# Scores of a wide attention as eight products in 32x64 tiles instead of four in 32x128 tiles

## The chip, the cores and the metric

The kernel runs on one core of a Trainium2 chip. The metric is the device time of one launch in microseconds (us). The core has five engines with instruction streams of their own: TensorE (PE, matrix products), VectorE (DVE), ScalarE (ACT), GpSimd (POOL) and SyncE (SP, used here to issue transfers). The profile splits TensorE's work into PE, the products, and PEld, the loads of the stationary operand that stand in front of each product.

## The reference

The program computes two attentions over the same 2048 x 576 input and mixes them by a gate. Attention A is recurrent: 64 segments of 32 rows, each with 8 rows of memory ahead of it, and the memory for the next segment is the first 8 rows of this segment's output. Attention B is wide: 32 heads of width 18, all 2048 queries against all 2048 keys.

```python
def _A_ref(x, mem0, Wq, Wk, Wv, Wo, seg_len):
    mem = mem0
    for s in range(n_seg):                       # 64 segments, one after the other
        h = jnp.concatenate([mem, x[:, s * seg_len:(s + 1) * seg_len, :]], axis=1)
        q, k, v = ...                            # 576 -> 32 heads x 128
        p = _softmax(jnp.where(mask, q k^T * scale, -1e9))
        o = (p v) Wo
        mem = o[:, :M, :]                        # M = 8
        outs.append(o[:, M:, :])

def _B_ref(x, wqkv, wo):
    scores = jnp.einsum('bhqd,bhkd->bhqk', q, k) * scale     # 32 heads, width 18
    p = _softmax(scores, axis=-1)
    o = jnp.einsum('bhqk,bhkd->bhqd', p, v)
    return o.transpose(0, 2, 1, 3).reshape(B, S, D) @ wo

g = _sigmoid((x * gate_w).sum(-1, keepdims=True))
return g * a + (1 - g) * b
```

## The kernel before

**The wide attention, B.** Heads go in groups of four (`GB` = 8 groups), each padded from 18 to 32 rows, so that four heads fill 128 partitions. Queries go in chunks of `QC` = 512, keys in blocks of 128. One such pair of a query chunk and a key block, for four heads, is a *visit*; there are 8 x 4 x 16 = 512 of them (loops over `gq` and `kb`, from line 915). A visit has three parts:

- `visit` (lines 926 to 935): four products, one for each head. Head j has its keys in rows 32j to 32j + 31 of `kch` and its queries in the same rows of `qch`. The stationary operand is 32 rows x 128 keys, the moving one 32 rows x 512 queries, and the result 128 keys x 512 queries. The array is used as four row tiles, `tile_position=(32 * j, 0)`, so the four products can be in it together. Heads 0 to 2 go to the three banks of the tile `sb` in PSUM (the accumulator memory), head 3 to a bank of its own, `sp`.
- `expo` and `expo4` (lines 939 to 945): ScalarE takes the exponential of `sb` (128 x 1536) and of `sp` (128 x 512) into `etb`.
- `values` (lines 950 to 960): four products in column tiles of 128 x 32, added up in `ob` over the sixteen key blocks of a query chunk.

There is one `sb` (three banks), one `ob`, and four banks `pb` that everything else shares, `sp` among them.

**The recurrent attention, A.** For each segment (loop from line 1242): projections to queries, keys and values in column tiles (`project`, products at line 1312, written to `pvv`), copies out of PSUM (`tm`), transposes by transfer (`tt`), scores (`psh`, lines 1426 and 1434), exponential, sums (`pss`), reciprocal (`rq`), a broadcast (`prb`), weighted values (`pso`, line 1500, tiles of 64 x 128), output projection (`acc`, line 1194) and the fold back to the next memory (`pw`). The last rows of segments are projected in units of four banks (`last_unit`, lines 1025 and 1029), and dummy products keep the array busy (`warm_col`, line 902).

**What sets the order.** The class `Plan` holds every piece of work with its engines, an assumed duration and a priority, and works out one order for each engine before a program exists. The visits are put in between the steps of the recurrence. The piece named `sb` (line 937) has the assumed duration 0.3, the mode "row", and takes the default of 4 pairs for the planner's count of instructions. The change touches the body of `visit` alone, so the planner sees the same pieces with the same numbers and every engine keeps its order.

Of the kernel before, what the change touches and what calls it, by code (L numbers as in the profile page):

```python
# [110 lines left out]
class Plan:  # L111
# [59 lines left out]
    def add(  # L171
        self, name, engs, dur, fn, deps=(), prio=5.0, mode=None, take=(), give=(), tail=0.0, dmas=0, kb=0.0,
        use=None, pairs=4, alt=None, waits=0.0,
    ):
        op = Op(name, engs, dur, fn, deps, prio, mode, take, give, tail)
        op.dmas, op.kb = dmas, kb
        op.pairs, op.alt, op.form, op.waits = pairs, alt, mode, waits
        op.kind = self.kinds.setdefault(kind_of(name), len(self.kinds))
        op.use = self.ARRAY.get(mode) if use is None else use
        op.seq = len(self.ops)  # L180
        op.slots = {}
        self.ops.append(op)
        return op
# [193 lines left out]
def kernel(  # L377
# [15 lines left out]
    nc = tc.nc  # L393
    P = nc.NUM_PARTITIONS
# [77 lines left out]
    for j in range(4):  # L472
        r = slice(32 * j, 32 * j + 32)
# [52 lines left out]
    def bank(shape, dt, name, k=0):  # L526
        return ps_a.tile(shape, dt, name=name, tag=f"pb{plan.slot('pb', k)}")

    def given(pool, tag, shape, dt):
        k = plan.slot(tag)  # L530
        return pool.tile(shape, dt, name=tag, tag=f"{tag}{k}", bufs=1)
# [332 lines left out]
    def load_k(c):  # L864
        g, kc = divmod(c, NQC)
        use = visits.get(("kuse", c - NKR))


        def fn(e):
            by_head(ktd, g, slice(kc * QC, (kc + 1) * QC), kring[c % NKR], False, queue(e))  # L870

        k_of[c] = add(f"lk{c}", *carrier(4, c >= 4), fn, [use, z_k[c % NKR], *stores_for(1, g, [kc]), weight_loads["wk"][-1] if c >= 4 else None], prio=0.6, dmas=4, kb=90)

    def load_v(c):
        g, kc = divmod(c, NQC)
        use = visits.get(("vuse", c - NVR))
        hf = g // (GB // 2)

        def fn(e):
            queue(e)(  # L880
                out=vring[c % NVR][:, :].rearrange("p (k f) -> p k f", f=P),
                in_=vgd[hf][4 * kc:4 * kc + 4][:, :, g % (GB // 2), :].rearrange("k p f -> p k f"),
            )

        deps = [v_stores[hf * NKB + kb] for kb in range(4 * kc, 4 * kc + 4)]
        v_of[c] = add(f"lv{c}", *(("POOL", 0.77) if c >= 4 else carrier(1, False)), fn, [use, *deps, weight_loads["wk"][-1] if c >= 4 else None], prio=0.65, dmas=1, kb=128)

    def load_q(i):
        g, qc = divmod(i, NQC)
        use = visits.get(("quse", i - NQR))  # L890

        def fn(e):
            by_head(qtd, g, slice(qc * QC, (qc + 1) * QC), qring[i % NQR], False, queue(e))

        q_of[i] = add(f"lq{i}", *carrier(4, i >= 2), fn, [use, z_q[i % NQR], *stores_for(0, g, [qc]), weight_loads["wk"][-1] if i >= 2 else None], prio=0.55, dmas=4, kb=90)
# [19 lines left out]
    for gq in range(GB * NQC):  # L915
        RANK.update(RANKS[gq // 8])
        g, qc = divmod(gq, NQC)
        load_q(gq)
        for kb in range(NKB):
            c = 4 * g + kb // KC  # L920
            o = (kb % KC) * P
            if qc == 0 and kb % KC == 0:
                load_k(c)
                load_v(c)

            def visit(e, c=c, gq=gq, o=o, kb=kb):
                box["sb", gq, kb] = sb = ps_s.tile([P, 3, QC], FP32, name="sb")
                box["sp", gq, kb] = sp = bank([P, QC], FP32, "sp")
                kc, qt_ = kring[c % NKR], qring[gq % NQR]
                for j in range(4):  # L930
                    r = slice(32 * j, 32 * j + 32)
                    nc.tensor.matmul(  # L932
                        sb[:, j, :] if j < 3 else sp[:, :], lhsT=kc[r, o:o + P], rhs=qt_[r, :], start=True, stop=True,
                        tile_position=(32 * j, 0),
                    )

            vi = add(f"sb{gq}.{kb}", "PE", 0.3, visit, [k_of[c], q_of[gq], last_vi], prio=-0.6 if gq < 2 else 0.0, mode="row", take=("sb", "pb"))

            def expo(e, gq=gq, kb=kb):
                box["etb", gq, kb] = etb = given(bint, "etb", [P, 4, QC], BF16)  # L940
                nc.scalar.activation(out=etb[:, 0:3, :], in_=box["sb", gq, kb][:, :, :], func=ACT.Exp, scale=scale_b)  # L941

            def expo4(e, gq=gq, kb=kb):
                etb = box["etb", gq, kb]
                nc.scalar.activation(out=etb[:, 3, :], in_=box["sp", gq, kb][:, :], func=ACT.Exp, scale=scale_b)  # L945

            ex = add(f"ex{gq}.{kb}", "ACT", act_time(1536), expo, [vi], prio=0.0, take=("etb",), give=(("sb", vi, 0),))
            ey = add(f"ey{gq}.{kb}", "ACT", act_time(512), expo4, [ex], prio=0.01, give=(("pb", vi, 0),))

            def values(e, c=c, gq=gq, kb=kb, o=o):  # L950
                if kb == 0:
                    box["ob"] = ps_o.tile([P, QC], FP32, name="ob")
                ob, vc, etb = box["ob"], vring[c % NVR], box["etb", gq, kb]
                for j in range(4):
                    nc.tensor.matmul(  # L955
                        ob[32 * j:32 * j + 32, :], lhsT=vc[:, o + 32 * j:o + 32 * j + 32], rhs=etb[:, j, :],
                        start=(kb == 0), stop=(kb == NKB - 1), tile_position=(0, 32 * j), skip_group_check=True,
                    )
                if kb == NKB - 1:
                    box["ob", gq] = ob  # L960

            va = add(
                f"ob{gq}.{kb}", "PE", 0.216, values, [ex, ey, v_of[c], last_va], prio=-0.5 if gq < 2 else RANK["ob"], mode="col",
                take=("ob",) if kb == 0 else (), give=(("etb", ex, 0),),
            )
            visits[gq, kb] = (vi, ex, va)
            last_vi, last_va = vi, va
            if kb == 0:
                plan.opens.add(va)
            if kb == NKB - 1:  # L970
                plan.closes.add(va)
            if kb == 0:
                first_va = va
            if kb == NKB - 1:
                visits["quse", gq] = vi
            if qc == NQC - 1 and kb % KC == KC - 1:
                visits["kuse", c], visits["vuse", c] = vi, va

        NBK = QC // 32

        def f_turn(e, gq=gq):
            box["tq", gq] = tq = bint.tile([P, NBK, 32], FP32, name="tq")
            nc.vector.transpose(out=tq[:, :, :].rearrange("p b e -> p (b e)"), in_=box["ob", gq][:, :])

        def f_rec(e, gq=gq):
            box["rtb", gq] = rtb = bint.tile([P, NBK, 1], FP32, name="rtb")
            nc.vector.reciprocal(out=rtb[:, :, :], in_=box["tq", gq][:, :, DhB:DhB + 1])

        def f_mul(e, gq=gq):
            box["tn", gq] = tn = bint.tile([P, NBK, 32], BF16, name="tn")  # L990
            nc.vector.tensor_tensor(
                out=tn[:, :, :], in0=box["tq", gq][:, :, :],
                in1=box["rtb", gq][:, :, :].to_broadcast([P, NBK, 32]), op=ALU.mult,
            )

        def f_back(e, gq=gq):
            box["stage", gq] = stage = bint.tile([P, QC], BF16, name="stage", bufs=2)
            nc.vector.transpose(out=stage[:, :], in_=box["tn", gq][:, :, :].rearrange("p b e -> p (b e)"))  # L998

        prev = fin_state.get("back")  # L1000
        f1 = add(f"ft{gq}", "DVE", 0.7, f_turn, [va, prev], prio=0.5, give=(("ob", first_va, 0),))
        f2 = add(f"fr{gq}", "DVE", 0.26, f_rec, [f1], prio=RANK["fin"])
        f3 = add(f"fm{gq}", "DVE", 0.7, f_mul, [f2], prio=RANK["fin"])
        store2 = stages.get(gq - 2)
        f4 = add(f"fb{gq}", "DVE", 0.7, f_back, [f3, store2], prio=RANK["fin"])
        fin_state["back"] = f4
        if gq < GB * NQC - 1:
            def f_store(e, gq=gq, g=g, qc=qc):
                by_head(otd, g, slice(qc * QC, (qc + 1) * QC), box["stage", gq], True, queue(e))

            stages[gq] = add(f"fs{gq}", *carrier(4, True), f_store, [f4], prio=0.9, dmas=4, kb=90)
        else:
            stages[gq] = f4
# [696 lines left out]
    for n in range(NT):  # L1710
        qc, i = divmod(n, 4)
# [84 lines left out]
```

## Time and profile before

| | |
|---|---|
| time, median of 3 runs | 1423.44 us (1421.48 to 1425.37) |
| the profiled execution | 1421.8 us, of which the span on the core is 1420.0 us |
| PE busy | 1345.2 us, 95% of the span |
| ACT busy | 1091.4 us, 77% |
| DVE busy | 848.2 us, 60% |
| POOL busy | 535.4 us, 38% |
| products of `visit` | 2048, 386 ns each in the profile |
| granted TensorE clock, mean | 0.992 |

Busy time of PE is the union of overlapping products, and the end of a product is modelled, so that 386 ns of one product is not what it takes from the array: the distance from one start to the next is. A line of the groups names the line of the kernel, the engine, the operation, output and inputs by their names, the tile of the array (rows*columns), the shape and the count; then busy time, mean duration of one, and what the engine waited for just before. A line of the timeline gives the start, the length and how many instructions were merged.

### The profile page before, as it was taken

Reading aid. Unit: us, or ns where it says so; the run is one execution under the profiler, and the core shown is the slowest. Engines: PE = TensorE matmul, PEld = TensorE weight load, DVE = VectorE, ACT = ScalarE, POOL = GpSimd, SP = SyncE. Lnnn points to the kernel's source line nnn. Section 1 sums busy time; section 2 is a strip of 40 time slices with the busy share of each in tenths; the row PEclk is TensorE's granted clock in tenths of the full one; section 3 lists DMA queues with packets and bytes.
Section 4 is the critical chain, followed back from the end, with each engine's and each line's share of the span. In section 5 each row is a group of like instructions: output and inputs, shape, how many; then the busy total and the mean of one; then the engine's idle time right before and its main releaser. Section 6 shows DMA issues by size and latency. Waiting matters only on the chain. (4 is left out here: it accounts for less than half of the span.)

```text
span 1420.0 us, 74484 instructions
## 1 busy us (share of the span) xinstructions
PE 1345.2 (95%) x33172; PEld 720.4 (51%) x33184; DVE 848.2 (60%) x2019; ACT 1091.4 (77%) x1277; POOL 535.4 (38%) x1162
## 2 busy tenths in 40 slices
PE   7999899999999999999999999999999999999998
PEld 4555344555554545555555544555554545444545
DVE  4443466665565566656666655656656665665566
ACT  3477688888887787887887888787778788887884
POOL 7352154334532346332543425333354324521310
PEclk9999999999999999999999999999999999999999
DMA  8787544333433344333433334333335333333335
GB/s 251 253 314 220 131 87 75 64 68 69 82 62 64 60 79 76 76 61 65 85 67 70 69 66 76 68 62 69 65 80 89 60 54 59 72 56 53 56 81 169
DMA packets 343997, 130.73 MB, mean 92 GB/s; under 512 B 296495, under 2 KB 330023, under 8 KB 343675
## 3 DMA queue, kind: packets, MB, share of 16 engines
q1 hardware_dynamic: 315155, 80.47, 29.2%
q0 software_dynamic: 26368, 43.31, 11.4%
q8 instruction: 259, 4.24, 1.3%
q10 hardware_dynamic: 2152, 2.19, 0.5%
q14 instruction: 63, 0.52, 0.1%
HBM read 52.74 MB, written 31.12 MB: 59 GB/s over the span
## 5 line engine op out<-in xcount | busy, mean ns | idle before, releaser
L941 ACT ACTIVATE etb<-sb 128x1536 bf16<-128x1536 f32 x512 | 743.5, 1452 | 227.5 <-PE sp L932 153.0
L540 DVE CAST tm<-pvv 128x512 bf16<-128x512 f32 x358 | 246.3, 688 | 230.3 <-PE pvv L1312 228.3
L945 ACT ACTIVATE etb<-sp 128x512 bf16<-128x512 f32 x512 | 305.0, 596 | 4.8 <-PE sp L932 4.8
L1312 PEld LDWEIGHTS <-ht 128*32 128x32 bf16 x7680 | 202.8, 96 | 196.2 <-issue 21.6
L932 PE MATMUL sb<-qch,kch 32*128 32x512 bf16 x1536 | 201.8, 386 | 3.2 <-ACT etb L941 1.8
L932 PE MATMUL sp<-qch,kch 32*128 32x512 bf16 x512 | 197.6, 386 | 7.6 <-DVE vl L540 5.8
L955 PE MATMUL ob<-etb,vch 128*32 128x512 bf16 x2048 | 201.9, 387 | 0.3 <-issue 0.3
L1194 PE MATMUL acc<-wo,ot 128*32 128x288 bf16 (+1 forms) x6144 | 165.7, 248 | 7.3 <-issue 3.6
L1312 PE MATMUL pvv<-wq_m,ht 128*32 128x512 bf16 x2048 | 142.1, 380 | 3.9 <-DVE ht L1559 1.5
L1312 PE MATMUL pvv<-wv_m,ht 128*32 128x512 bf16 x2048 | 141.7, 380 | 0.3 <-DVE tm L540 0.2
L1312 PE MATMUL pvv<-wk_m,ht 128*32 128x512 bf16 x2048 | 140.5, 380 | 0.1
L1194 PEld LDWEIGHTS <-ot 128*32 128x32 bf16 x6144 | 112.7, 97 | 47.0 <-DVE ot L540 17.7
L540 DVE CAST ot<-pso 128x320 bf16<-128x320 f32 x200 | 91.6, 484 | 58.3 <-PE pso L1500 57.3
L932 PEld LDWEIGHTS <-kch 32*128 32x128 bf16 x2048 | 54.5, 91 | 137.0 <-issue 121.7
L1411 DVE COPY qk<-tt 128x512 bf16<-128x512 bf16 x256 | 79.9, 314 | 54.5 <-DMA tt<-tm 51.2
L1261 POOL COPY ht<-xg 128x96 bf16<-128x96 bf16 x64 | 17.7, 277 | 236.8 <-PE pvv L1312 230.5
L955 PEld LDWEIGHTS <-vch 128*32 128x32 bf16 x2048 | 53.6, 94 | 73.5 <-issue 62.5
L851 POOL DMA_DIRECT2D qch<-qtd x120 | 61.7, 521 | 68.3 <-PE sp L932 64.6
L851 POOL DMA_DIRECT2D otd<-stage x124 | 62.8, 513 | 65.0 <-DVE stage L998 38.6
L540 DVE CAST vl<-pv 128x512 bf16<-128x512 f32 x84 | 57.2, 685 | 38.8 <-PE pv L1025 21.8
L1489 DVE TENSOR_TENSOR et<-et,prb 128x320 bf16<-128x320 bf16 x128 | 61.6, 484 | 28.0 <-PE prb L1478 23.1
L1444 ACT ACTIVATE et<-psh 128x320 bf16<-128x320 f32 x128 | 56.6, 445 | 27.0 <-PE psh L1434 25.7
(161 smaller groups left out, 1968.1 us busy)
## 6 DMA issues: line engine op xcount, KB each, us to landing
xl<-qkd SPq DMA_DIRECT2D x64, 128.0 KB
v_sb<-tm SPq DMA_DIRECT2D x256, 32.0 KB
qkd<-vl POOLq DMA_DIRECT2D x48, 128.0 KB, 2.5
wo<-in_A_Wo_dram POOLq DMA_DIRECT2D x4, 1152.0 KB, 10.9
vgd<-vt SPq DMA_DIRECT2D x32, 128.0 KB
wv_m<-in_A_Wv_dram POOLq DMA_DIRECT2D x4, 1024.0 KB
wq_m<-in_A_Wq_dram POOLq DMA_DIRECT2D x4, 1024.0 KB, 9.2
wk_m<-in_A_Wk_dram POOLq DMA_DIRECT2D x4, 1024.0 KB
```

The source lines that it names most:

```text
L540: nc.vector.tensor_copy(out=out_of(), in_=in_of())
L851: dma(out=rows_, in_=pads) if out else dma(out=pads, in_=rows_)
L932: nc.tensor.matmul(sb[:, j, :] if j < 3 else sp[:, :], lhsT=kc[r, o:o + P], rhs=qt_[r, :], start=True, stop=True, tile_position=(32 * j, 0),)
L941: nc.scalar.activation(out=etb[:, 0:3, :], in_=box["sb", gq, kb][:, :, :], func=ACT.Exp, scale=scale_b)
L945: nc.scalar.activation(out=etb[:, 3, :], in_=box["sp", gq, kb][:, :], func=ACT.Exp, scale=scale_b)
L955: nc.tensor.matmul(ob[32 * j:32 * j + 32, :], lhsT=vc[:, o + 32 * j:o + 32 * j + 32], rhs=etb[:, j, :], start=(kb == 0), stop=(kb == NKB - ...
L1194: nc.tensor.matmul(acc[32 * q:32 * q + 32, :], lhsT=o[:, slot, t0:t0 + CT], rhs=wo[:, h, d:d + n], start=(first and s_ == (s_ % 2 if wide ...
L1261: nc.gpsimd.tensor_copy(out=ht[:, 0:NF, M:CT], in_=xg[:, 0:NF, t])
L1312: nc.tensor.matmul(pv[32 * j:32 * j + 32, :], lhsT=ht[:, cc, :], rhs=rw, start=(c == 0), stop=(c == NF), tile_position=(0, 32 * j), skip_g ...
L1411: eng.tensor_copy(out=opened["qk"][:, hf, a, 0:16 * L].rearrange("p (j i t) -> p j i t", i=4, t=L)[:, :, :, 0:CT], in_=box["tt", s, a, hf] ...
L1444: nc.scalar.activation(out=opened["et", hf][:, :], in_=box["psh", s, hf][:, :], func=ACT.Exp, scale=scale_a)
L1489: nc.vector.tensor_tensor(out=et[:, :], in0=et[:, :], in1=box["prb", s, hf][:, :], op=ALU.mult)
```

## The change

The four products of a visit become eight. The 128 keys of a block are taken in two halves of 64: the outer loop goes over the halves, the inner one over the four heads. Each product has a stationary operand of 32 rows x 64 keys, the same moving operand of 32 x 512 queries as before, and writes 64 partitions of the bank that its head had before. The array is used as eight tiles of 32 x 64, `tile_position=(32 * j, i)`. What is computed, where it ends up, the tiles in memory and the order of all pieces are the same. `skip_group_check=True` tells the program builder not to compare the two halves' accumulation groups; it is no instruction.

```diff
-                for j in range(4):
-                    r = slice(32 * j, 32 * j + 32)
-                    nc.tensor.matmul(
-                        sb[:, j, :] if j < 3 else sp[:, :], lhsT=kc[r, o:o + P], rhs=qt_[r, :], start=True, stop=True,
-                        tile_position=(32 * j, 0),
-                    )
+                for i in range(0, P, 64):
+                    for j in range(4):
+                        r = slice(32 * j, 32 * j + 32)
+                        nc.tensor.matmul(
+                            sb[i:i + 64, j, :] if j < 3 else sp[i:i + 64, :], lhsT=kc[r, o + i:o + i + 64], rhs=qt_[r, :],
+                            start=True, stop=True, tile_position=(32 * j, i), skip_group_check=True,
+                        )
```

## The prediction

> **What bounds the kernel now.** I read the page's busy shares first, then the costliest groups, then the stages, then who waits for the changed line, and last the timeline of one visit.
>
> ```profile
> PE 1345.2 (95%) x33172; PEld 720.4 (51%) x33184; DVE 848.2 (60%) x2019; ACT 1091.4 (77%) x1277; POOL 535.4 (38%) x1162
> ...
> L932 PE MATMUL sb<-qch,kch 32*128 32x512 bf16 x1536 | 201.8, 386 | 3.2 <-ACT etb L941 1.8
> L932 PE MATMUL sp<-qch,kch 32*128 32x512 bf16 x512 | 197.6, 386 | 7.6 <-DVE vl L540 5.8
> L955 PE MATMUL ob<-etb,vch 128*32 128x512 bf16 x2048 | 201.9, 387 | 0.3 <-issue 0.3
> ```
>
> TensorE is full. The stages say the same: from 150 to 1350 us it is busy 1150.5 of 1200 us, so only 49.5 us are idle in the body. The changed products start almost without a wait (3.2 and 7.6 us in 512 visits), so what they take is taken from the bounding engine. From the list of waits:
>
> ```profile
> PE psh L1434 <- DVE qk L1411: 10.5, 24, 1.0
> PE prb L1478 <- DVE rq L1470: 8.3, 20, 1.0
> ...
> PE sb L932 <- ACT etb L941: 1.8, 8, 0.4
> ```
>
> The columns are total us, times, longest. PE waits for ScalarE's exponentials 8 times in 512 visits; the other way round ScalarE waits 293 times, 153.0 us, for `sp`. ScalarE is no bound. The stretch of one visit in the timeline gives the price that counts, start to start:
>
> ```profile
> 700.90 0.39 PE L1312 MATMUL pvv<-wq_t,ht 128*32 128x512 bf16 x4
> 701.22 0.10 PEld L932 LDWEIGHTS <-kch 32*128 32x128 bf16 x4 [0.42 <-issue]
> 701.22 0.39 PE L932 MATMUL sb<-qch,kch 32*128 32x512 bf16 x3
> 701.23 0.38 PE L932 MATMUL sp<-qch,kch 32*128 32x512 bf16 x1
> ...
> 701.55 1.05 PE L1312 MATMUL pvv<-wk_m,ht 128*32 128x512 bf16 x16
> ...
> 702.42 0.39 PE L1312 MATMUL pvv<-wk_t,ht 128*32 128x512 bf16 x4
> ...
> 702.64 0.39 PE L955 MATMUL ob<-etb,vch 128*32 128x512 bf16 x4
> ```
>
> Four products of 512 columns in four column tiles take 0.22 us when the next round has the same tile form (702.42 to 702.64). Where the form changes they take 0.32 (700.90 to 701.22), and a visit's round 0.33 (701.22 to 701.55). So the four products of a round do run together, and a change of form costs about 0.1 us on either side of a visit. The trace's own starts inside the round are 3.3 ns apart, tile after tile, in row and in column form.
>
> One more resource matters, since the change adds instructions. The view of the transfers has the program's own loading, and the timeline shows one place where it is late:
>
> ```profile
> q8 instruction: 259, 4.24, 1.3%
> ```
>
> ```profile
> 366.77 0.42 PE L1194 MATMUL acc<-wo,ot 128*32 128x288 bf16 x5
> 368.07 0.55 PE L1194 MATMUL acc<-wo,ot 128*32 128x288 bf16 x11 [0.88 <-issue]
> ```
>
> 4.24 MB in 259 transfers is 16.4 KB each; over TensorE's 66,400 records it is 64 bytes for one. So this queue carries TensorE's program, 256 instructions at a time. The bracket is TensorE in the middle of a sum, waiting for nothing but its next instructions. Numbered in order, the starts with such a gap fall on the same place in each 256. Measured from one such place to the next, a block of 256 took 4.64 us in the median, one in four took under 4.02, one in twenty under 3.55, and the shortest 3.07. Starts of these transfers are never under 3.28 us apart, one in ten under 3.62. That is the pace at which blocks arrive, and TensorE already runs near it in places.
>
> **What the Trainium skill says.** "TensorEngine Tiling (Array Packing)", Key Properties: different tiles load and multiply in parallel, and changing the form drains the array. The trace agrees: 0.22 against 0.32 us. "TensorE: Matmul & The Clock Gate", Measured speedup vs the span model: each further tile adds about 4 ns, up to sixteen tiles of 32x32; the trace has 3.3 ns for four, and no 32x64 tile. The same page, Weight-path perf modes: a fast weight load needs a stationary operand of all 128 columns. The trace agrees in form, since before, the 128 columns are read as 4 chunks of 32. "Runtime: NRT & Kernel Launch", Terms: instruction memory is refilled in 16 KiB blocks; the trace has 16.4 KB.
>
> **The change part by part.**
>
> *Arithmetic.* None is removed. Eight tiles of 32x64 fill the same array as four of 32x128, for the same 512 columns: 213 ns at full clock. Cost 0 if all eight stream together.
>
> *Starts.* Four more pairs in a visit, at 3.3 ns: the last starts 13.3 ns later. The whole round ends later by that, and so does what follows.
>
> *Weights.* After a change of form the loads can't run ahead. The view has no 64-column load. Behind a change, a round of 32-column loads delays its first round by 10 ns (226 against 216 ns to the next), and the 128-column loads in four chunks end alike. Sixty-four columns without chunks are twice 32, so an estimate is 10 ns more. Bounds: 0, if the pairs' 13 ns cover it, and 40, if a column took 1/1.2 ns as the skill's clock page has it in LDWEIGHTS (53 ns for 64, less 13 now); the trace's 10 ns for 32 columns speaks against the latter. I take 10.
>
> *Change of form.* Still one ahead of and one behind each visit. From the last start to the next form's first load, less the streaming, the trace has 91 to 95 ns after column tiles, 94 after the full array, 99 after these row tiles (86 in some), 87 after 64x128. Neither fewer columns nor fewer rows shortens it by more than some ns, so I take 0; bounds -27 ns (64 columns fewer to cross at 2.4 a ns) and +10.
>
> *Sum for one visit.* 13.3 + 10 + 0 = 23.3 ns. The stages of the changed line put 156 of its 2056 load records, 39 visits, ahead of 150 us, where transfers have a share of 0.79 and 0.84 and TensorE waits for them; I count nothing there. 473 x 23.3 ns = 11.0 us.
>
> *Program.* 512 visits x 8 records = 4096 instructions, 16 more blocks on 259, at 6% more instructions for each us. I laid 8 more starts into each visit in the trace's own list of starts, moved what follows by 30 ns, and added up by how much blocks of 256 fall short of the refill's pace. At a pace of 3.6 us the list of before is short by 2.8 us and the new one by 11.2, so 8.4 more; at 3.5 us it is 1.5 and 7.4, so 6 more; at 3.8 us 7.9 and 23.2, so 15 more. I take 8. Low end 2: products already queued cover shortfalls under 0.2 us.
>
> *Who waits.* ScalarE's exponential starts some 25 ns later, within its 227.5 us of idle time ahead of line 941. If that cover went, 512 x 25 ns = 12.8 us would lie on ScalarE. Queued behind the visit on TensorE are the recurrence's projections and `ob`; they come late by the same amount. SP's and POOL's orders are untouched. DVE's copies only wait longer for `pvv` (228.3 us already).
>
> *What is absorbed.* Where TensorE then waits for DVE anyway, a longer visit shortens the wait. `psh` waits in 24 of 128 cases, `prb` in 20 of 128, other lines more rarely. I take 12% of 11.0 + 8, so 2.3 us.
>
> Sum: 11.0 + 8 - 2.3 = 16.7 us. The profiled execution is 1421.8 us (span 1420.0 and 1.8 around it) and would be 1438.5. The median of the runs is 1.6 us above that execution: 1423.4 + 16.7 = **1440 us**.
>
> **Rivals.**
>
> *The two halves don't stream together.* Both halves of a head need the same 32 rows. If their products excluded each other, each visit would take a second round: 512 x 0.216 = 110.6 us, so 1534 us. For it: no tile of this form is in the trace. Against it: column tiles share all 128 rows among four products, start 3.3 ns apart and finish a round in 0.216 us; the skill's sixteen tiles split rows and columns at once.
>
> *Nothing that can be measured.* The starts are covered by the change of form, the program's loading keeps up, and the rest goes into TensorE's 49.5 us of idle time: under 4 us, 1424 to 1427. For it: the absolute numbers are small, and blocks take 4.64 us in the median. Against it: those 49.5 us are spread over 1200, while the visits are everywhere.
>
> *Faster.* The drain could be shorter for a tile of 64 columns, on the side behind the visit. At the bound, -27 ns, the visit would gain 3.7 ns (13.3 + 10 - 27), 2 us in all. To win it must be shorter by more than the 23.3 ns and what the program's loading costs, 8 us over 473 visits or 17 ns: from about 40 ns on. At 60 ns less, 20 ns x 473 = 9 us, so 1414 us. Against it: 91 to 99 ns after four different forms.
>
> **How the numbers follow.** A measurement of this kernel tells about 0.3%, 4.3 us, from no change. My forecast, 1428 and up without a second round, has 0.76; two rounds 0.06; no measurable change 0.10; faster 0.08. So slower is 0.82. In the forecast's own case the low ends (13.3 ns a visit and 2 us of loading, less 12%) give 7 us, 1431, and the high ends (13.3 + 40 + 10 ns and 15 us, less 12%) 40 us, 1463; both high at once is unlikely. The range is 1426 to 1458: it leaves out two rounds, faster, part of no change, and a few hundredths above.
>
> **What would show it.** Line 932 should be 4096 products of tile 32*64, with starts about 3.3 ns apart. From a visit's first start to the next form's first start there should be about 0.35 us instead of 0.33; 0.54 would be two rounds, 0.30 a shorter drain. The instruction queue should carry 275 transfers, and "issue" should show more idle time ahead of lines 1194, 1312, 1434 and 1500, on products without a wait of their own. ACT and DVE busy times should stay. I am wrong if the visit's price is unchanged, if the blocks cost nothing, or if the waits for DVE shrink by as much as the visits grow.

## The result, and the profile after

The median went from 1424.4 us (four runs, 1421.48 to 1429.11) to 1443.09 us (four runs, 1440.49 to 1448.58): a ratio of 1.0133, 95% interval 1.0092 to 1.0174, or 18.7 us slower. The profiled execution after took 1448.6 us (span 1446.8), 5.5 us above that median.

The page of the changed kernel: busy shares, the instruction queue, and the groups of the changed line (now 933; everything below the edit stands one line lower).

```profile
PE 1361.7 (94%) x35219; PEld 738.6 (51%) x35232; DVE 846.8 (59%) x2019; ACT 1093.8 (76%) x1277; POOL 535.4 (37%) x1162
...
q8 instruction: 275, 4.51, 1.4%
...
L933 PE MATMUL sb<-qch,kch 32*64 32x512 bf16 x3072 | 224.3, 400 | 7.5 <-DMA kch<-ktd 4.5
L933 PE MATMUL sp<-qch,kch 32*64 32x512 bf16 x1024 | 213.5, 399 | 4.4 <-DVE vl L540 4.2
```

The eight tiles are there (32*64, 3072 + 1024 products), and the program takes 275 blocks. The busy times of DVE, ACT and POOL stay within 3 us. TensorE has 16.5 us more busy time in a span that is 26.8 us longer, so it also stands still longer. This is the timeline of the same visit as before the change, the 250th:

```profile
714.97 0.39 PE L1313 MATMUL pvv<-wq_t,ht 128*32 128x512 bf16 x4
715.29 0.41 PE L933 MATMUL sb<-qch,kch 32*64 32x512 bf16 x3
715.30 0.40 PE L933 MATMUL sp<-qch,kch 32*64 32x512 bf16 x1
715.30 0.41 PE L933 MATMUL sb<-qch,kch 32*64 32x512 bf16 x3
715.32 0.40 PE L933 MATMUL sp<-qch,kch 32*64 32x512 bf16 x1
715.64 1.05 PE L1313 MATMUL pvv<-wk_m,ht 128*32 128x512 bf16 x16
```

Both halves start within 0.03 us and share one round; ahead of the visit the change of form takes the same 0.32 us, behind it the next form starts 0.35 us after the visit's first product in place of 0.33. Over all 512 visits the trace's own starts give, from the first product to the next form's first load, a median of 350 ns in place of 323. Those 27 ns are 13 of later starts (first to last product 23 in place of 10) and 14 from the last start to the next form (327 in place of 313). I call this the visit's price.

The list of TensorE's waits holds the waits for the next instructions, marked "issue". First the largest of them before, then the list after:

```profile
PE acc L1194 <- issue: 3.6, 2, 2.8
```

```profile
PE psh L1435 <- DVE qk L1412: 9.2, 20, 1.2
PE prb L1479 <- DVE rq L1471: 9.1, 18, 1.2
PE acc L1195 <- issue: 6.2, 10, 1.6
...
PE sb L933 <- ACT etb L942: 1.4, 6, 0.3
```

All lines marked "issue" come to 5.1 us before and to 13.4 us after. TensorE waits for ScalarE's exponential (`etb`) only 6 times, so ScalarE is still no bound.

Each weight load outside the visits has its counterpart in the other trace, in the same order (31,136 of them), so I compared the gaps between them. The profiled execution after is 26.5 us longer from the first to the last: 14.9 us in gaps that hold a visit, 11.5 us in the others. Of the latter, those after 150 us come to 12.6 us: +17.2 us in stretches of twelve records, each at a border between two blocks of 256, -5.0 us where a border lay before, and 0.4 us everywhere else. Such a stretch holds 4.7% of the starts. Laying the stretches a little differently moves these sums by about 1 us. So outside the visits the loss lies at the borders. The waits say the same: if weight loads, products and semaphore records are numbered together, all 19 of this trace's "issue" waits after 160 us end at places 192 to 195 of a block of 256. In all twelve traces of this case together it is 168 of 168.

### The profile page after: what moved, and what is told of

It is laid out like the page before. It is cut to its first block, busy times and chain, and to the rows that moved or that the text cites. A ratio compares the mean times of both kernels' runs of the same rounds, so it can differ in the third digit from the quotient of the medians.

```text
span 1446.8 us, 78579 instructions
## 1 busy us (share of the span) xinstructions
PE 1361.7 (94%) x35219; PEld 738.6 (51%) x35232; DVE 846.8 (59%) x2019; ACT 1093.8 (76%) x1277; POOL 535.4 (37%) x1162
## 5 line engine op out<-in xcount | busy, mean ns | idle before, releaser
L942 ACT ACTIVATE etb<-sb 128x1536 bf16<-128x1536 f32 x512 | 743.8, 1453 | 253.3 <-PE sp L933 183.5
L933 PE MATMUL sb<-qch,kch 32*64 32x512 bf16 x3072 | 224.3, 400 | 7.5 <-DMA kch<-ktd 4.5
L933 PE MATMUL sp<-qch,kch 32*64 32x512 bf16 x1024 | 213.5, 399 | 4.4 <-DVE vl L540 4.2
L933 PEld LDWEIGHTS <-kch 32*64 32x64 bf16 x4096 | 70.7, 101 | 148.0 <-issue 130.5
```

The source lines that it names most:

```text
L933: nc.tensor.matmul(sb[i:i + 64, j, :] if j < 3 else sp[i:i + 64, :], lhsT=kc[r, o + i:o + i + 64], rhs=qt_[r, :], start=True, stop=True, t ...
```

## The experiments

Ten runs were made besides the two. A ratio is to the kernel before in the same sitting. The sittings differ by up to 0.8% (the median of the kernel before was 1415.5 to 1427.1 us in the three of them), so sums over whole traces from different sittings are compared with care, and ratios decide. Microseconds given after a ratio are worked out from it; where the two medians differ by another amount, that is given too.

**Instructions without tiles: `halves`.** Eight products again, but in the old form, with each head's queries taken as two halves (against the kernel before).

```diff
-                for j in range(4):
-                    r = slice(32 * j, 32 * j + 32)
+                for h in range(0, QC, 256):
+                    for j in range(4):
+                        r, q = slice(32 * j, 32 * j + 32), slice(h, h + 256)
...
+                            sb[:, j, q] if j < 3 else sp[:, q], lhsT=kc[r, o:o + P], rhs=qt_[r, q],
+                            start=True, stop=True, tile_position=(32 * j, 0), skip_group_check=True,
```

> Eight products in a visit as after the change, but in the old row tiles of 32x128: each head's 512 queries are taken as two halves of 256 columns. The instructions grow by the same 4096, the tiles don't change. Theory (half of the loss is the program's loading, the other half the tiles): a visit's price, start to next form's start, stays within 5 ns of 323, so under 2.5 us; the loading costs 6 to 14 us as in the changed kernel, less a little that waits take up. Expected 8 to 12 us over before, ratio 1.006 to 1.008, with 275 transfers of instructions and issue waits of some 10 us in place of 5. Rival (all of the loss lies in the form of the tiles, 26 us over 512 visits is 52 ns each): no change beyond 2 us, ratio under 1.002.

Measured: 1444.57 us, ratio 1.0134 (1.0111 to 1.0156), 19 us (17.5 by the medians). The visit's price is 325 ns, 2 more than before or 1.0 us in all. This stretch of its timeline shows it from 711.11 to 711.43. The waits for instructions add up to 15.2 us, of which the second view has the largest part:

```profile
710.78 0.39 PE L1313 MATMUL pvv<-wq_t,ht 128*32 128x512 bf16 x4
711.11 0.28 PE L933 MATMUL sb<-qch,kch 32*128 32x256 bf16 x3
711.12 0.28 PE L933 MATMUL sp<-qch,kch 32*128 32x256 bf16 x1
711.23 0.27 PE L933 MATMUL sb<-qch,kch 32*128 32x256 bf16 x3
711.24 0.27 PE L933 MATMUL sp<-qch,kch 32*128 32x256 bf16 x1
711.43 1.05 PE L1313 MATMUL pvv<-wk_m,ht 128*32 128x512 bf16 x16
```

```profile
PE acc L1195 <- issue: 6.5, 12, 1.5
```

So some 17 us come from 4096 more instructions alone, about twice what I had expected of them. Outside the visits its starts are 15.6 us later at borders of blocks. Some 7 us more lie elsewhere outside the visits; the kernel before was also 5.3 us slower in this sitting (1427.1 us) than in the trace that it is compared with (1421.8 us). The rival, that all lies in the tiles, falls.

**Visits' price without instructions: `ninetysix`.** The other way round: four products, with a longer load of the stationary operand.

```diff
+                if "sb" not in box:
+                    box["sb"] = ps_s.tile([P, 3, QC], FP32, name="sb")
+                box["sb", gq, kb] = sb = box["sb"]
...
+                    w = 96 if j < 3 and (gq or kb) else P
-                        sb[:, j, :] if j < 3 else sp[:, :], lhsT=kc[r, o:o + P], rhs=qt_[r, :], start=True, stop=True,
+                        sb[0:w, j, :] if j < 3 else sp[:, :], lhsT=kc[r, o:o + w], rhs=qt_[r, :], start=True, stop=True,
```

> The kernel before with four products in a visit and not one instruction more, but three of the four stationary operands have 96 columns in place of 128 (the last quarter of the keys is left out for three heads, after the first visit; the tile sb is one tile for good, so that these rows hold old scores). 96 columns are no longer read in four chunks. If loading goes column by column at 2.4 a ns, it takes 40 ns in place of 13, so the visit's price is 350 ns as in the changed kernel, without its instructions. Theory (the visit's price costs what it is, less what waits take up): 11 to 14 us over before. Rival (the loading of the program alone makes the loss, a visit's 27 ns go into waits): under 5 us. If the price stays at 323, the chunks aren't what the changed kernel lost.

Measured: ratio 1.0038 (1.0024 to 1.0052), 5.4 us, with 22 runs of it. The price is 347 ns, 24 more than before, and the instruction queue carries 259 transfers as before. The page's groups show the form, and that its products hardly wait:

```profile
L935 PE MATMUL sb<-qch,kch 32*96 32x512 bf16 (+1 forms) x1536 | 215.7, 412 | 3.8 <-ACT etb L944 1.9
```

512 x 24 ns = 12.3 us, of which 5.4 (3.4 to 7.4) arrive at the end. Neither expectation was met: the visits do cost, but some 55% of their price goes, where the prediction took off 12%. Where it goes stays open. TensorE's waits other than for instructions are 45.2 us here and 55.4 in the trace of before, but the two are from different sittings, and this profiled execution (1415.64 us) was itself 5.4 us under the median of its runs.

**Where the borders lie: `shift48` and `shift128`.** The kernel before, with products of one column at the gate that move all later instructions; the second kernel has 128 in place of 48.

```diff
+        for k in range(48):
+            nc.tensor.matmul(pgs[:, 0:1], lhsT=xT[:, 0, 0:P], rhs=gw[:, 0:1], start=True, stop=True)
```

> The kernel before with 48 more products of one column, at the gate (about 50 us after the start), each written over by the gate's own products. They cost 48 x 26 ns = 1.2 us of TensorE where they stand and move every later instruction by 96 places against the blocks of 256 in which the program is loaded. Theory (loading stalls where a block is used up in less than about 3.5 us): replaying the starts of before with boundaries moved by 96 gives 12.1 us of shortfall in place of 1.5 at a pace of 3.5 us, so 10 us more; with the 1.2 us and what waits take up, 7 to 12 us over before, ratio 1.005 to 1.008. Rival (where the blocks' borders lie doesn't matter): at most the 1.2 us, ratio under 1.001.

> The same with 128 more products: 128 x 26 ns = 3.3 us where they stand, and 256 places, so the borders of the blocks fall on the same instructions as before. Theory: no more shortfall than before, so between 0 and 3.5 us over before, and less than the one with 48, though 80 products more are in it. Rival (instructions cost by their number alone): more than the one with 48.

Measured: with 48, ratio 1.0066 (1.0041 to 1.0092), 9.4 us (7.8 by the medians); with 128, ratio 1.0034 (1.0011 to 1.0057), 4.8 us (2.6 by the medians). In the traces, gaps after 150 us grew by 13.8 us with 48 and by 1.4 us with 128, where the rest of the loss lies ahead of 150 us, at the gate itself. So eighty more of these products cost less, as the theory has it: they leave the borders on the same instructions. The intervals of the two ratios overlap; the traces tell them apart. With 48, "issue" waits after 160 us number 14 in place of 4. They still end at places 192 to 195, which now means at other instructions. From the two lists of waits, with 48 first:

```profile
PE psh L1436 <- issue: 2.6, 2, 1.4
PE pv L1031 <- issue: 2.0, 3, 0.9
```

```profile
PE pgs L815 <- issue: 2.5, 1, 2.5
PE pv L1031 <- issue: 0.5, 1, 0.5
```

The 2.5 us in the second are at the gate, where 128 products in a row wait for the next block. I had expected at most 3.5 us of this kernel and had not thought of this wait; whether the limit was passed depends on the measure (4.8 or 2.6 us).

**Which part of the tile costs: `sixteen`.** Sixteen tiles of 32x32 (against the changed kernel).

```diff
-                for i in range(0, P, 64):
+                for i in range(0, P, 32):
-                            sb[i:i + 64, j, :] if j < 3 else sp[i:i + 64, :], lhsT=kc[r, o + i:o + i + 64], rhs=qt_[r, :],
+                            sb[i:i + 32, j, :] if j < 3 else sp[i:i + 32, :], lhsT=kc[r, o + i:o + i + 32], rhs=qt_[r, :],
```

> Sixteen products of 32 rows x 32 keys in a visit. Starts: twelve more than before at 3.3 ns, so the last starts 50 ns after the first in place of 10 (before) and 23 (after the change). Weights: if the 14 ns that the changed kernel has between the last start and the next form's first load, over the old form, come from loading 64 columns one by one, 32 columns give 313 ns again (as before) and the visit's price is 363 ns; if any column tile has them, 327 stays and the price is 377 to 380. On 473 to 512 visits that is 19 to 29 us. Program: 12288 more instructions, 48 more blocks; replaying the starts at a pace of 3.5 to 3.6 us for a block gives 24 to 32 us more. Expected 40 to 60 us over before, 1465 to 1485 us. Rival (the tiles alone): 20 to 29 us, 1445 to 1453.

Measured: 1479.76 us, ratio 1.0392 (1.0363 to 1.0421), 56 us (52.7 by the medians). One visit of its trace, without the products in between:

```profile
728.82 0.39 PE L933 MATMUL sb<-qch,kch 32*32 32x512 bf16 x3
...
728.87 0.38 PE L933 MATMUL sp<-qch,kch 32*32 32x512 bf16 x1
729.18 1.05 PE L1313 MATMUL pvv<-wk_m,ht 128*32 128x512 bf16 x16
```

The price is 363 ns in the median, and from the last start to the next form it takes 313 ns, as with the old tiles. So a tile of fewer columns doesn't cost these 14 ns as such. That they are the changed kernel's 64 columns, loaded one by one, fits this run; loading and draining were not measured apart. The visits' 40 ns come to 20 us at most. So more than half of the 56 us is again the program, as the expectation had it; its 307 blocks have waits for instructions of 22.9 us.

**The order of the tiles: `inner`** (against the changed kernel).

```diff
-                for i in range(0, P, 64):
-                    for j in range(4):
+                for j in range(4):
+                    for i in range(0, P, 64):
```

> The changed kernel with the two loops of a visit exchanged: the two halves of a head stand one after the other, so two tiles on the same 32 rows start back to back. Theory (each further tile 3.3 ns, the columns' loading 14 ns, whatever the order): a visit's price of 350 ns, 1440 to 1446 us, within 4 us of the changed kernel. Rival (tiles on the same rows hold each other up): the price rises by 14 ns and more.

Measured: 1437.77 us, ratio 1.0161 (1.0131 to 1.0191), price 350 ns. In that sitting the kernel before took 1415.5, so this is 22 us more; the interval overlaps that of the changed kernel. The time itself is under the 1440 to 1446 us expected, in a sitting whose kernel before was 9 us faster than in the first. Two tiles on the same 32 rows that start back to back don't hold each other up: the price is the same.

**The changed kernel again: `again`.**

> The changed kernel once more, beside the others: 16 to 21 us over before. Theory: where the shortfall at the blocks' borders lies differs from one execution to the next by some us, since the refills' pace does, while the visits' price of 350 ns doesn't.

Measured: ratio 1.0147 (1.0111 to 1.0183), 21 us (21.9 by the medians), at or just above the upper end of what was expected; price 350 ns. At the borders its gaps are 8.6 us longer than before, where the first profiled execution had 12.5; in `inner` it is 7.6. In these three executions the price is the same and the borders vary.

**Both with a program made shorter: `lean_four`, `lean_eight`, `lean_halves`.** Half of the recurrent scores are left out, which takes away as many instructions as the change adds; the visits are those of before, of the change, and of `halves`.

```diff
-                for r in range(8):
+                for r in range(0, 8, 2):
                     for i in range(4):
                         k, o = (i // 2) * 8 + r, 32 * (i % 2)
```

> The kernel before with every other step of the recurrent scores left out (16 of the 32 score products of each of 128 pieces; those heads keep the mask's values alone, so this part of the result is missing). It has 2048 products and as many weight loads less, 16 blocks of the program less, which is what the change adds. Expected 10 to 25 us under before: at most 2048 x 11 ns of the array, and fewer waits for the program. It is the base for the next run.

> The changed kernel with the same part left out, so its number of instructions is that of the kernel before. Theory (two prices that add: 27 ns for each visit and the loading): the loading is relieved, the visits' price is still there, so 12 to 16 us over lean_four, with a visit's price of 350 against 323 ns. Rival (the loading alone decides, and a longer visit only takes up time that the loading would have taken): under 6 us over lean_four.

> lean_four (half of the recurrent scores left out) with the visits as eight products of 256 columns in row tiles of 32x128, so the instructions of lean_eight at a visit's price of some 326 ns. Theory: with the program's loading relieved the 4096 instructions cost little, 1 to 5 us over lean_four, and the 11.5 us of lean_eight over lean_four are the price of its visits. Rival (what lean_eight lost is still loading): as much as lean_eight, 9 to 14 us over lean_four.

Measured, against the kernel before: `lean_four` 0.9958 (0.9943 to 0.9973), `lean_eight` 1.0034 (1.0017 to 1.005), `lean_halves` 1.0008 (0.9989 to 1.0026). `lean_four` is 5.7 us under before; I had expected 10 to 25, and why it is less stays open. `lean_eight` is 11.5 us over `lean_four` in the same sitting, a little under the 12 to 16 expected. `lean_halves`, from another sitting, is over `lean_four` by 1.0008 / 0.9958 = 1.0050, some 7 us, with an uncertainty of about 3.4 us from the two intervals. That lies between its two expectations. The same 4096 instructions cost less in the shorter program (19 us for `halves` falls to 7). What is left of `lean_eight`'s 11.5 us for the form of its tiles is the ratio of its ratio to that of `lean_halves`, 1.0026 or 3.7 us, with an uncertainty of some 3.5 us; that agrees with the 5.4 us of `ninetysix`. The traces don't show what the 7 us are: at borders the lean kernels' gaps differ by 1 to 2 us only, and the profiled executions of `lean_four` and `lean_halves` by 1.8 us in all.

## Why the prediction was right, and where it was not

The sum was 16.7 us and the result 18.7; 1440 stands against 1443.09, inside 1426 to 1458. The sign and the two causes, a longer visit and more instructions to load, hold. That the sum came within 2 us is luck: what the program costs was put at about half, what is absorbed of the visits' price was put much too low, and the two errors offset each other in part. The two later sets of runs of this form (`again`, `inner`) came to 21 and 23 us.

- **Arithmetic and tiles: right.** Eight tiles stream together; the second round (1534 us) didn't come, and exchanging the loops leaves the price at 350 ns.
- **Starts: right.** 13.3 ns were forecast and 13 measured.
- **Weights: right within 4 ns.** I took 10 of a range from 0 to 40; it is 14. It goes with the columns: 32 (`sixteen`) give nothing over the old form, 64 give 14, and 96 in three of four loads (`ninetysix`) give 21. From 32 to 64 columns the Trainium skill's figure in "TensorE: Matmul & The Clock Gate", LDWEIGHTS, would be an estimate of 27 ns; the measured 14 decides.
- **Change of form: right at 0, as far as can be seen.** None of the forms that were run starts the next form sooner than 313 ns after its last product of 512 columns. Only loading and drain together were measured, so a shorter drain that a longer load hides is not excluded.
- **Sum for one visit: 23.3 ns forecast, 27 measured.** The 39 visits ahead of 150 us, which I left out, are not free: the gaps that hold them grew by 2.8 us in the profiled execution and by 0.8 in `again`, where 39 x 27 ns is 1.1.
- **Program: mechanism right, size too small.** I took 8 us. In the profiled execution the borders cost 12.5 us, and without longer visits (`halves`) the instructions alone cost about 17. My replay of the trace's starts used one pace for all refills (transfers of a block); at 3.8 us it gave 15, which I had put at the upper end. The changed kernel's borders (7.6 to 12.5 us with `again` and `inner`) are below the 15.6 of `halves`; that a longer visit gives a refill time is the reason I would give, and it is only argued.
- **What is absorbed: 12% forecast, too little.** Of the visits' price alone, 12.3 us, only 5.4 remained. In the changed kernel the two prices together, some 17 and 5.4, come near the 19 to 23 us of its three ratios (`again` and `inner` included).
- **Who waits: right.** ScalarE's idle time ahead of its exponential rose from 227.5 to 253.3 us, and the exponential's busy time stayed. The two pages, before first:

```profile
L941 ACT ACTIVATE etb<-sb 128x1536 bf16<-128x1536 f32 x512 | 743.5, 1452 | 227.5 <-PE sp L932 153.0
```

```profile
L942 ACT ACTIVATE etb<-sb 128x1536 bf16<-128x1536 f32 x512 | 743.8, 1453 | 253.3 <-PE sp L933 183.5
```

- **Rivals.** "Nothing that can be measured" had the idle time take it all up. About half of one price didn't arrive at the end (`ninetysix`), the rest and the loading did. "Faster" needed a drain shorter by 40 ns; the time from the last start to the next form grew by 14.

So the split I gave, 9.7 us for visits and 7 for the program after absorption, is wrong: alone, they cost 5.4 and about 17. The larger part of the loss is the number of instructions and not the form of the tiles: `halves`, with the old tiles, has a ratio of 1.0134, and the three sets of runs with the new tiles have 1.0133, 1.0147 and 1.0161.

## What to carry to other kernels

On a full TensorE, count instructions as well as columns: splitting a product can add next to nothing to the array's time (2 ns a visit in `halves`) and still cost more through the loading of the program than a new form of tiles does. Where a list of waits shows "issue" in the middle of a sum, number TensorE's records, semaphore records included, and see whether the gaps fall on one place in each block. If they do, the position of the borders is part of the kernel's tuning, and any edit that adds or removes instructions ahead moves it. Behind a change of form, loads of 64 and 96 columns delayed the next form by 14 and 21 ns here, and loads of 32 columns did not.

## What the runs showed of the hardware that I had not expected

- Here places mattered more than number: 96 instructions early in the program cost 9.4 us, 256 at the same point 4.8 (7.8 and 2.6 by the medians).
- In the changed kernel a start held up at a border mostly comes 2.3 to 2.9 us after a refill's start, and the next refill mostly begins 1.0 to 1.3 us after that start. From one refill to the next it is never less than 3.3 us (3.28 us in the kernel before).
- Behind a change of form, the time from the last start to the next form is 313 ns for 32 columns, 327 for 64 and 334 where three of the four loads have 96, and 313 for 128 read in four chunks.
